# Moving the last 64 rows of a Gram product onto column tiles of TensorE, and its column sums onto four narrower ones

## The chip, the cores and the metric

The kernel runs on one core of a Trainium2 chip. Of its engines, TensorE multiplies matrices and writes the products to a memory called PSUM; VectorE, ScalarE and GpSimd work by element, and VectorE and ScalarE copy results out of PSUM; SyncE's queue issues transfers between memories (DMA). The metric is the device time of one execution in microseconds (us).

## The reference, cut to what matters

```python
B, S, D, H, F = 1, 2048, 576, 32, 4608          # Dh = D // H = 18
xn = layernorm(x)
q, k, v = split(xn @ wqkv)                      # by head
pq, pk = phi(q), phi(k)                         # phi(t) = (t+1 if t > 0 else exp(t)) + 1e-6
kv  = einsum("bhsd,bhse->bhde", pk, v)
z   = einsum("bhsd->bhd", pk)
o   = einsum(pq, kv) / (einsum(pq, z) + 1e-6)
out = x + o @ wo + (gelu(xn @ w_gate) * (xn @ w_up)) @ w_down
```

The kernel does not form v. It uses pk^T v = (pk^T xn) wv. So it accumulates the Gram product G = xn^T pk (576 x 576) over 16 token tiles of 128 tokens, and multiplies by wv later (kv stage). The stretch in which k and pk are computed, one token tile after another, with a part of G accumulated alongside, is called the K stage; a query unit is five matmuls that compute a piece of q. The sum of pk over tokens, z, is one more row of such a product, with a column of ones for xn.

## The kernel before

576 rows are four blocks of 128 and a last block of 64. The column of ones follows the 64, so the last block has 65 weight columns. A matmul takes weights of up to 128 columns (`lhsT`); a block of 65 leaves half the columns of the array empty and takes as long (0.25 us per token tile for 577 columns of pk in three pieces, by the prediction's reading below, where two full pieces with 577 columns take 2 x 0.1235).

```python
G_A = {   # row block: (bank, column, first column of pk, width); runs inside the K stage
    0: [(0, 0, 0, 288), (1, 0, 288, 289)],
    1: [(2, 0, 0, 288), (3, 0, 288, 289)],
    4: [(0, 288, 0, 224), (1, 289, 224, 223), (2, 288, 447, 130)],
}
G_B = {2: [(5, 0, 0, 288), (6, 0, 288, 289)], 3: [(0, 0, 0, 288), (1, 0, 288, 289)]}

def g_accumulate(n, pieces):
    for kt, ps_ in pieces.items():
        j0, m = (kt * P, P) if kt < 4 else (D, HP + 1)
        for b, col, d0, w in ps_:
            nc.tensor.matmul(ps_all[:m, b, col:col + w], lhsT=xn[:, n, j0:j0 + m], rhs=pk[:, n, d0:d0 + w], ...)

# ... after the K stage:
for n in range(NS): g_accumulate(n, {2: G_B[2]})
g_copy(4, ...); g_copy(0, ...); g_copy(1, ...)
# ... the last query steps, q_unit(12)
for n in range(NS): g_accumulate(n, {3: G_B[3]})
g_copy(2, ...); g_copy(3, ...)
q_unit(13)
z_stage(2, 3)       # spreads z over each head's rows, for the denominators
kv_stage(6, 5)      # G times wv
```

Then follow row-tiled pairs (two matmuls over 64 rows of the array side by side): query units, gate and up, and three pairs for the denominators (`den_pair`). A pair swaps its two PSUM banks halfway; an empty instruction on another queue, a "turn", passes the word. For the denominators that queue is SyncE's.

Of the kernel before, what the change touches and what calls it, by code (L numbers as in the profile page):

```python
# [8 lines left out]
ACT = mybir.ActivationFunctionType  # L9
ALU = mybir.AluOpType  # L10
BF16 = mybir.dt.bfloat16
F32 = mybir.dt.float32
# [3 lines left out]
P = 128  # L16
HP = 64
S = 2048
D = 576
# [3 lines left out]
NS = S // P  # L23
# [4 lines left out]
HALF = D // 2  # L28
KT = 5
# [3 lines left out]
CR = 7 * DH  # L33
EPS_LN = 1e-5
EPS_ATT = 1e-6
# [2 lines left out]
WDS = 3  # L38
NWARM = 38
TD = 4  # L40
XW = 642
PKW = 578


class _Ring:
# [11 lines left out]
def kernel(  # L57
# [11 lines left out]
    nc = tc.nc  # L69
# [8 lines left out]
    const = ctx.enter_context(tc.tile_pool(name="const", bufs=1))  # L78
# [6 lines left out]
    ps_all = psum.tile([P, 8, 512], F32, name="ps_all")  # L85
# [10 lines left out]
    apool = attn_cm.__enter__()  # L96
# [5 lines left out]
    wqkv_sb = apool.tile([P, KT, 3 * D], BF16, name="wqkv_sb")  # L102
# [4 lines left out]
    def load_w(which, on=nc.sync):  # L107
        c = slice(which * D, (which + 1) * D)
        on.dma_start(wqkv_sb[:, 0:4, c], A_wqkv[0:512, c].rearrange("(kt p) c -> p kt c", p=P))
        on.dma_start(wqkv_sb[0:HP, 4, c], A_wqkv[512:576, c])  # L110
        if which == 0:
            on.dma_start(wq_lo[HP:P, :], A_wqkv[512:576, c])

    nc.scalar.preload_act_table_set("natural_log_exp_and_others")  # L114
    load_x(0, 1)
# [3 lines left out]
    nc.vector.memset(wqkv_sb[HP:P, 4, :], 0.0)  # L119
    nc.vector.memset(wqkv_sb[0:1, 0, D:D + 2], 0.0)  # L120
    load_w(1, nc.scalar)

    ident = const.tile([P, P], BF16, name="ident")
# [29 lines left out]

    pk = h_store[:, 0:NS * PKW].rearrange("p (n d) -> p n d", n=NS)
    wg_bufs = _Ring([fpool.tile([P, 4, GUB * P], BF16, name=f"wg{i}") for i in range(NWBUF)])
# [5 lines left out]
    def load_gu(i, part):  # L161
# [15 lines left out]


    xn = apool.tile([P, NS, XW], BF16, name="xn")
    nc.gpsimd.memset(xn[:, :, 640:641], 1.0)  # L180
    nc.gpsimd.memset(pk[:, :, D:D + 1], 1.0)

    bmask = const.tile([P, CR], F32, name="bmask")
    bm3 = bmask[:].rearrange("p (h e) -> p h e", e=DH)
# [2 lines left out]
        out=bm3, in_=bm3, compare_op=ALU.is_ge, fill=0.0,  # L187
# [3 lines left out]
        out=bm3, in_=bm3, compare_op=ALU.is_ge, fill=0.0,  # L191
        base=DH - 1, pattern=[[DH, 7], [0, DH]], channel_multiplier=-1,
    )
    g_sb = apool.tile([P, KT, D], BF16, name="g_sb")
    nc.gpsimd.memset(g_sb[HP:P, 4, :], 0.0)

    zsel = const.tile([P, CR], BF16, name="zsel")
    nc.gpsimd.memset(zsel[:], 0.0)
    nc.gpsimd.memset(zsel[HP:HP + 1, :], 1.0)

    mv = persist.tile([P, NS, nc.vector.BN_AGGR_DIM], F32, name="mv")
    rstd = persist.tile([P, NS], F32, name="rstd")
# [36 lines left out]
    def k_bank(n, hf):  # L239

        return hf if n == 1 else 5 + hf
# [9 lines left out]
    def phi_tile():  # L251
        return awork.tile([P, D], F32, name="phi_e", tag="phi_e", bufs=6)


    k_e = {}

    def k_part(n, hf):
        if n not in k_e:
            k_e[n] = phi_tile()
        hs = slice(hf * HALF, (hf + 1) * HALF)  # L260
        return ps_all[:, k_bank(n, hf), :HALF], k_e[n][:, hs], pk[:, n, hs]

    def k_relu(n, hf):
        ps, e, _ = k_part(n, hf)
        nc.scalar.activation(out=e, in_=ps, func=ACT.Relu, scale=-1.0)  # L265

    def k_exp(n, hf):
        _, e, _ = k_part(n, hf)
        nc.scalar.activation(out=e, in_=e, func=ACT.Exp, scale=-1.0)  # L269

    def k_sum(n, hf):
        ps, e, out_ = k_part(n, hf)
        nc.vector.scalar_tensor_tensor(out=out_, in0=ps, scalar=0.0, in1=e, op0=ALU.max, op1=ALU.add)  # L273
# [1 line left out]


    G_A = {
        0: [(0, 0, 0, 288), (1, 0, 288, 289)],
        1: [(2, 0, 0, 288), (3, 0, 288, 289)],
        4: [(0, 288, 0, 224), (1, 289, 224, 223), (2, 288, 447, 130)],  # L280
    }
    G_B = {2: [(5, 0, 0, 288), (6, 0, 288, 289)], 3: [(0, 0, 0, 288), (1, 0, 288, 289)]}
    eps_sum = const.tile([P, KT], F32, name="eps_sum")

    def g_accumulate(n, pieces):
        for kt, ps_ in pieces.items():
            j0, m = (kt * P, P) if kt < 4 else (D, HP + 1)
            for b, col, d0, w in ps_:
                nc.tensor.matmul(  # L289
                    ps_all[:m, b, col:col + w], lhsT=xn[:, n, j0:j0 + m], rhs=pk[:, n, d0:d0 + w],  # L290
                    start=(n == 0 and col == 0), stop=(n == NS - 1), skip_group_check=True,
                )



# [2 lines left out]
    LO, HI = slice(0, HP), slice(HP, P)  # L298
# [37 lines left out]
    def q_unit(i):  # L336
        sc, c = divmod(i, NCH)
        rows = DH * HCH[c]
        q0 = DH * HOFF[c]
        ps = ps_all[:rows, q_banks.next(), :]  # L340
        for kt in range(KT):
            nc.tensor.matmul(  # L342
                ps, lhsT=wqkv_sb[:, kt, q0:q0 + rows], rhs=xnT[:, kt, sc * SC:(sc + 1) * SC],
                start=(kt == 0), stop=(kt == KT - 1),
            )
        q_out[i] = ps
# [57 lines left out]
    def mask_pair(dst, b4, b1):  # L404

        nc.vector.tensor_tensor(
            out=dst[:CR, 0:4, :], in0=ps_all[:CR, b4, 0:4 * CR].rearrange("p (c d) -> p c d", c=4),
            in1=bmask[:CR, :].unsqueeze(1).to_broadcast([CR, 4, CR]), op=ALU.mult,
        )
        r4 = DH * HCH[4]  # L410
        nc.vector.tensor_tensor(
            out=dst[:r4, 4, :r4], in0=ps_all[:r4, b1, 0:r4], in1=bmask[:r4, :r4], op=ALU.mult,
        )

    def chunk_out(c, b4, b1):
        rows = DH * HCH[c]
        return ps_all[:rows, b4, c * CR:c * CR + rows] if c < 4 else ps_all[:rows, b1, 0:rows]

    def z_stage(b4, b1):
        for c in range(NCH):  # L420
            rows = DH * HCH[c]
            nc.tensor.matmul(
                chunk_out(c, b4, b1), lhsT=g_sb[:, 4, c * CR:c * CR + rows], rhs=zsel[:, :rows],
                start=(c in (0, 4)), stop=True, skip_group_check=True,
            )
        mask_pair(zrep, b4, b1)

    def kv_stage(b4, b1):

        for kt in (0, 1, 4, 2, 3):  # L430
            for c in range(NCH):
                rows = DH * HCH[c]
                nc.tensor.matmul(  # L433
                    chunk_out(c, b4, b1), lhsT=wqkv_sb[:, kt, 2 * D + c * CR:2 * D + c * CR + rows],
                    rhs=g_sb[:, kt, c * CR:c * CR + rows],
                    start=(kt == 0 and c in (0, 4)), stop=(kt == 3), skip_group_check=True,
                )
        mask_pair(kvT, b4, b1)

# [29 lines left out]
    def den_norm(sc, c, q, pieces):  # L469
# [30 lines left out]
        (lambda n: k_sum(n, 0), [9.00, 16.55, 13.07, 15.61, 18.43, 21.08, 23.93, 26.99, 30.05]),  # L500
        (lambda n: k_sum(n, 1), [10.83, 11.19, 13.68, 16.19, 18.79, 21.44, 24.29, 27.35, 30.41]),
        (lambda n: g_accumulate(n, G_A), [11.96, 17.36, 18.24, 20.21, 21.09, 23.07, 26.12, 29.18, 32.24]),
    ]

# [27 lines left out]
    todo += [(4.0, lambda n: nc.vector.memset(x_sb[0:1, n, 0:2], 0.0), 4)]  # L532
    todo += [(4.01, lambda n: load_x(n, 4), n) for n in (4,)]
    todo += [(4.02, lambda n: load_w(0), 0)] + [(4.03, lambda n: load_x(n, 4), n) for n in (8, 12)]
    todo.sort(key=lambda x: x[0])

# [2 lines left out]
        step(n)  # L539


    def g_copy(kt, pieces, on):

        m = P if kt < 4 else HP + 1
        eps = eps_sum[:m, kt:kt + 1]
        b, col, _, w = pieces[kt][-1]
        nc.vector.tensor_scalar_mul(out=eps, in0=ps_all[:m, b, col + w - 1:col + w], scalar1=EPS_ATT)
        for (b, col, d0, w), eng in zip(pieces[kt][::-1], on):
            w = min(w, D - d0)
            out_, in_ = g_sb[:m, kt, d0:d0 + w], ps_all[:m, b, col:col + w]  # L550
            if eng is nc.scalar:
                nc.scalar.activation(out=out_, in_=in_, func=ACT.Identity, bias=eps, scale=1.0)
            else:
                nc.vector.tensor_scalar_add(out=out_, in0=in_, scalar1=eps)


    load_w(2)
    for i in range(NWBUF):
        load_gu(i, 0)
        load_gu(i, 1)  # L560
    for n in range(NS):
        g_accumulate(n, {2: G_B[2]})
    g_copy(4, G_A, (nc.vector, nc.scalar, nc.vector))
    g_copy(0, G_A, (nc.scalar, nc.vector))
    g_copy(1, G_A, (nc.scalar, nc.vector))
    for _, step, n in todo[tail:]:
        step(n)
    q_unit(12)
    for step in (q_exp1, q_min, q_max):
        step(12)  # L570
    for n in range(NS):
        g_accumulate(n, {3: G_B[3]})
    g_copy(2, G_B, (nc.scalar, nc.vector))
    g_copy(3, G_B, (nc.scalar, nc.vector))
    q_unit(13)
    z_stage(2, 3)
    kv_stage(6, 5)
    for step in (q_exp1, q_min, q_max):
        step(13)
# [161 lines left out]
```

## Time and profile before

| | kernel before |
|---|---|
| time, median of 3 (range) | 523.57 us (523.47 to 523.83) |
| span of the profiled run | 521.7 us |
| TensorE busy | 99% of the span |
| Gram product after the K stage | two rows of the chain, 4.75 us (with one token tile of the K stage) and 4.00 us |
| first Gram row after the K stage to the row-tiled pairs | 65.78 - 53.20 = 12.58 us |

The view that this document uses most is the chain of work that ended last, in order of time. Each row is a stretch that the next had to wait for: start, length, what, and how many instructions. I call the 12.58 us of the last line the **edited stretch**: all that the change does for TensorE after the K stage lies in it.

### The profile page before, as it was taken

What the parts mean: (1) busy time and instruction counts of PE and PEld (TensorE: products, weight loads), DVE (VectorE), ACT (ScalarE), POOL (GpSimd) and SP (SyncE); (2) the same over time, 40 slices, a digit from 0 to 9 for tenths busy, and PEclk for the clock granted to TensorE, in tenths of its full rate; (3) what the DMA queues carried; (4) which work ended last, traced back from release to release, by engine and by line L of the source; (5) the groups of instructions that cost most, each with busy time, mean ns of one, the idle gap of its engine ahead of it and who ended that gap; (6) DMA issues with size and microseconds to landing.
All of it is one profiled execution on the core that took longest, in us unless ns stands there. A gap on an engine that the chain in (4) does not pass through costs nothing.

```text
span 521.7 us, 10641 instructions
## 1 busy us (share of the span) xinstructions
PE 516.1 (99%) x4498; PEld 313.5 (60%) x4498; DVE 250.9 (48%) x436; ACT 143.1 (27%) x293; POOL 35.2 (7%) x55
## 2 busy tenths in 40 slices
PE   7999999999999999999999999999999999999997
PEld 6777755555587754444577744444777544445775
DVE  7996565876358323433388133333584233433101
ACT  6898442332320013323200032232000123322000
POOL 2021000211001100000012000000011000000000
PEclk9999999999999999999999999999999999999999
DMA  8334609899500045555300155555100355440000
GB/s 279 62 64 118 154 25 264 254 269 266 157 12 13 13 124 155 144 156 160 93 13 13 41 166 145 155 156 155 29 23 13 103 161 158 140 134 2 13 11 24
DMA packets 106282, 57.89 MB, mean 111 GB/s; under 512 B 13370, under 2 KB 105722, under 8 KB 106234
## 3 DMA queue, kind: packets, MB, share of 16 engines
q1 hardware_dynamic: 105626, 56.55, 38.8%
q8 instruction: 35, 0.57, 0.5%
q10 hardware_dynamic: 608, 0.66, 0.4%
q14 instruction: 13, 0.11, 0.1%
HBM read 52.86 MB, written 2.36 MB: 106 GB/s over the span
## 4 chain that ended last, share of the span: by engine, by line
PE 97%; DMA 1%; ACT 1%; DVE 0%; issue 0%
PE ps_all L313 55%; PE ps_all L677 27%; PE ps_all L289 4%; PE ps_all L682 4%; PE ps_all L245 3%; PE ps_all L342 3%; DMA wqkv_sb<-in_A_wqkv_dram 1%; PE ps_all L451 1%; PE ps_all L433 0%; PE ps_all L659 0%; ACT xnT L234 0%; ACT L114 0%; ACT phi_e L265 0%; ACT phi_e L269 0%; DVE hT L273 0%; DVE res L685 0%
## 5 line engine op out<-in xcount | busy, mean ns | idle before, releaser
L313 PE MATMUL ps_all<-xnT,wg 64*128 64x512 bf16 x1152 | 272.6, 376 | 0.0
L313 PE MATMUL ps_all<-xnT,wu 64*128 64x512 bf16 x1152 | 271.8, 376 | 0.0
L648 DVE TENSOR_TENSOR hT<-ps_all,gl 128x512 bf16<-128x512 f32 x144 | 99.5, 691 | 161.9 <-ACT gl L647 161.2
L647 ACT ACTIVATE gl<-ps_all 128x512 f32<-128x512 f32 x144 | 86.1, 598 | 314.3 <-PE ps_all L313 297.4
L313 PEld LDWEIGHTS <-wu 64*128 64x128 bf16 x1152 | 108.3, 94 | 66.3
L313 PEld LDWEIGHTS <-wg 64*128 64x128 bf16 x1152 | 108.3, 94 | 66.1
L677 PE MATMUL ps_all<-wd_sb,hT 128*128 128x288 bf16 x1152 | 147.0, 286 | 0.0
L677 PEld LDWEIGHTS <-hT 128*128 128x128 bf16 x1152 | 112.3, 98 | 30.6 <-issue 1.3
L475 DVE RECIPROCAL den_sb<-den_sb 126x128 f32<-126x128 f32 (+1 forms) x80 | 68.3, 911 | 0.5
L685 DVE TENSOR_TENSOR res<-ps_all,x_sb 128x288 bf16<-128x288 f32 x32 | 14.7, 458 | 88.0 <-PE ps_all L682 88.0
L313 PE MATMUL ps_all<-xnT,wr 64*128 64x512 bf16 x288 | 55.1, 376 | 0.0
L478 POOL TENSOR_TENSOR pqT<-pqT,den_sb 126x512 bf16<-126x512 bf16 (+3 forms) x25 | 24.2, 966 | 317.3 <-DVE den_sb L475 279.4
L682 PE MATMUL ps_all<-m_sb,pqT 126*128 126x288 bf16 (+1 forms) x160 | 24.9, 285 | 0.0
L313 PEld LDWEIGHTS <-wr 64*128 64x128 bf16 x288 | 14.4, 94 | 16.9 <-issue 0.7
L245 PE MATMUL ps_all<-wqkv_sb,xnT 128*128 128x288 bf16 x160 | 22.5, 286 | 0.9 <-DMA wqkv_sb<-in_A_wqkv_dram 0.8
L289 PE MATMUL ps_all<-hT,xn 128*128 128x288 bf16 (+4 forms) x176 | 22.4, 275 | 0.0
L289 PEld LDWEIGHTS <-xn 128*128 128x128 bf16 (+1 forms) x176 | 17.5, 102 | 4.1
L245 PEld LDWEIGHTS <-xnT 128*128 128x128 bf16 x160 | 15.4, 98 | 6.9 <-issue 1.4
L682 PEld LDWEIGHTS <-pqT 126*128 126x128 bf16 (+1 forms) x160 | 15.5, 97 | 4.1
L342 PE MATMUL ps_all<-xnT,wqkv_sb 128*126 128x512 bf16 (+1 forms) x70 | 17.4, 378 | 0.0
L273 DVE SCALAR_TENSOR_TENSOR hT<-ps_all,phi_e 128x288 bf16<-128x288 f32 x32 | 13.2, 450 | 4.6 <-ACT phi_e L269 4.0
L265 ACT ACTIVATE phi_e<-ps_all 128x288 f32<-128x288 f32 x32 | 12.9, 410 | 3.6 <-PE ps_all L245 2.1
(68 smaller groups left out, 173.8 us busy)
## 6 DMA issues: line engine op xcount, KB each, us to landing
wg<-in_B_w_gate_dram SPq DMA_DIRECT2D x72, 256.0 KB, 2.9
wu<-in_B_w_up_dram SPq DMA_DIRECT2D x72, 256.0 KB, 3.5
wd_sb<-in_B_w_down_dram SPq DMA_DIRECT2D x12, 432.0 KB, 4.6
wr<-in_B_w_gate_dram SPq DMA_DIRECT2D x72, 32.0 KB, 2.7
wr<-in_B_w_up_dram SPq DMA_DIRECT2D x72, 32.0 KB, 3.1
out_dram<-res SPq DMA_DIRECT2D x15, 144.0 KB, 1.8
x_sb<-in_A_x_dram SPq DMA_DIRECT2D x3, 576.0 KB, 7.1
wqkv_sb<-in_A_wqkv_dram SPq DMA_DIRECT2D x2, 576.0 KB, 4.7
```

The source lines that it names most:

```text
L245: nc.tensor.matmul(ps_all[:, k_bank(n, hf), :HALF], lhsT=xnT[:, kt, n * P:(n + 1) * P], rhs=wqkv_sb[:, kt, D + hf * HALF:D + (hf + 1) * HALF],
L273: nc.vector.scalar_tensor_tensor(out=out_, in0=ps, scalar=0.0, in1=e, op0=ALU.max, op1=ALU.add)
L289: nc.tensor.matmul(ps_all[:m, b, col:col + w], lhsT=xn[:, n, j0:j0 + m], rhs=pk[:, n, d0:d0 + w], start=(n == 0 and col == 0), stop=(n == ...
L313: return nc.tensor.matmul(self.outs[i], lhsT=self.lhs(i, rows, kt), rhs=self.rhs(i, rows, kt), start=start, stop=stop, skip_group_check=True,)
L342: nc.tensor.matmul(ps, lhsT=wqkv_sb[:, kt, q0:q0 + rows], rhs=xnT[:, kt, sc * SC:(sc + 1) * SC], start=(kt == 0), stop=(kt == KT - 1),)
L475: nc.vector.reciprocal(out=d[:, h:h + P], in_=d[:, h:h + P])
L478: nc.gpsimd.tensor_tensor(out=pqT[:rows, c, cols], in0=pqT[:rows, c, cols], in1=d, op=ALU.mult)
L647: nc.scalar.activation(out=gl[:], in_=ps_all[:, b[0], :], func=ACT.Gelu_apprx_tanh)
L648: nc.vector.tensor_tensor(out=hT[:, GUB * k + i, :], in0=ps_all[:, b[1], :], in1=gl[:], op=ALU.mult)
L677: nc.tensor.matmul(acc, lhsT=hT[:, f, j * P:(j + 1) * P], rhs=wd_sb[:, f, hs], start=(f == 0), stop=False,)
L682: nc.tensor.matmul(acc, lhsT=pqT[:rows, c, ts_], rhs=m_sb[:rows, c, hs], start=False, stop=(c == NCH - 1),)
L685: nc.vector.tensor_tensor(out=res[:, hs], in0=acc, in1=x_sb[:, n, hs], op=ALU.add)
```

## The change

The intent: the array time that 65 of 128 columns left unused. The third row block takes the place of the last one inside the K stage. The last 64 rows come after the K stage, on two column tiles of 64: one takes the first 288 columns of pk, the other the second 288, at the same time. z can't ride along as a 65th column, so it gets matmuls of its own, with ones as weights, on four column tiles of 32: tile g takes token tiles g, g+4, and so on. The four partial sums are added in the z stage, by four rows of ones in place of one.

```diff
-    4: [(0, 288, 0, 224), (1, 289, 224, 223), (2, 288, 447, 130)],
+    2: [(0, 288, 0, 224), (1, 289, 224, 223), (2, 288, 447, 132)],
     }
-G_B = {2: [...], 3: [...]}
+G_B = {3: [(5, 0, 0, 288), (6, 0, 290, 289)]}
+def g_last(bank):
+    for n in range(NS):
+        for hf in range(2):
+            nc.tensor.matmul(
+                ps_all[hf * HP:(hf + 1) * HP, bank, 0:HALF + 1], lhsT=xn[:, n, 4 * P:4 * P + HP],
+                rhs=pk[:, n, PK0[hf]:PK0[hf] + HALF + 1],
+                start=(n == 0), stop=(n == NS - 1), skip_group_check=True,
+            )
+def z_sums(b0):
+    for n in range(NS):
+        g = n % 4
+        for hf in range(2):
+            nc.tensor.matmul(
+                ps_all[g * ZQ:(g + 1) * ZQ, b0 + hf, 0:HALF], lhsT=z_ones[:], rhs=pk[:, n, PK0[hf]:PK0[hf] + HALF],
+                start=(n < 4), stop=(n >= NS - 4), skip_group_check=True,
+            )
...
-    for n in range(NS):
-        g_accumulate(n, {3: G_B[3]})
-    g_copy(2, G_B, (nc.scalar, nc.vector))
-    g_copy(3, G_B, (nc.scalar, nc.vector))
+    g_last(0)
+    z_sums(1)
+    g_copy(3, ...)
+    g_copy(4, ...)
+    z_copies(1)          # one half on ScalarE, one on VectorE
     q_unit(13)
     z_stage(2, 3)
```

Cut here: layout of pk with a column of ones behind each half, a second copy of 64 rows of wv (one transfer more on SyncE's queue), the memsets, the kv stage's order.

## The prediction

> **What bounds the kernel now.** I read first the busy shares on the page of the kernel before, then its chain of work that ended last, then the same chain in order of time around the place that the change edits.
>
> ```profile
> PE 516.1 (99%) x4498; PEld 313.5 (60%) x4498; DVE 250.9 (48%) x436; ACT 143.1 (27%) x293; POOL 35.2 (7%) x55
> ...
> PE 97%; DMA 1%; ACT 1%; DVE 0%; issue 0%
> ```
>
> TensorE is busy in 99% of the span and makes up 97% of the chain. The chain in order of time, from the end of the K stage (each row: start, length, what):
>
> ```profile
> 52.12 1.08 PE ps_all L342 x5
> 53.20 4.75 PE ps_all L289 x39
> 57.95 1.08 PE ps_all L342 x5
> 59.02 4.00 PE ps_all L289 x32
> 63.02 1.08 PE ps_all L342 x5
> 64.10 0.26 PE ps_all L422 x5
> 64.36 1.43 PE ps_all L433 x25
> 65.78 24.31 PE ps_all L313 x223
> ```
>
> L289 is the Gram product, L342 a query unit, L422 the z stage, L433 the kv stage, L313 the row-tiled pairs. Each row starts where the last one ends: no other engine and no DMA has a link here, and from 12.04 us on every link of the K stage is TensorE too (rows of L245, L289 x7 and L342 only). So the time answers to TensorE's own issue time, nanosecond for nanosecond, unless the change puts a wait on that chain.
>
> From the rows I take slot lengths, which are what counts (a matmul's own duration, 286 ns, overlaps its neighbours). Ten 288-column matmuls of L245 take 1.23 us: 0.1225 us each. The 32 of the row at 59.02 (16 of 288 and 16 of 289 columns) take 4.00: 0.125 each. Five of 512 columns take 1.08: 0.215 each. The row-tiled pairs take 24.31 / 223 = 0.109 each, half of a 512-column slot, so two row tiles really run side by side.
>
> The groups of L289 by shape show what the last 64 rows of the Gram matrix cost: three matmuls per token tile with 65 weight columns.
>
> ```profile
> L289 PE MATMUL ps_all<-hT,xn 128*128 128x289 bf16 x64 | 16.6, 287 | 0.0
> L289 PE MATMUL ps_all<-hT,xn 128*128 128x288 bf16 x64 | 16.6, 286 | 0.0
> ...
> L289 PE MATMUL ps_all<-hT,xn 128*65 128x223 bf16 x16 | 4.2, 259 | 0.0
> L289 PE MATMUL ps_all<-hT,xn 128*65 128x224 bf16 x16 | 4.1, 258 | 0.0
> L289 PE MATMUL ps_all<-hT,xn 128*65 128x130 bf16 x16 | 3.5, 222 | 0.0
> ```
>
> The chain gives seven L289 matmuls per token tile 0.745 us. Four of them are full pieces at about 0.1235; the other three are left with 0.745 - 0.494 = 0.25 us per token tile, 4.0 us in all. That half-empty array time is what the change is after.
>
> **What the Trainium skill says.** (1) "TensorEngine Tiling (Array Packing)", Tiling Modes, Key Properties: tiles run loads and matmuls in parallel, but changing the tiling mode drains TensorE. The trace agrees for row tiles: in the timeline of TensorE at the end of the first gate/up stage the last pair starts at 255.14, and the first full-array matmul only at 255.45, 0.31 us later instead of one slot of 0.213, so about 0.10 us goes to the switch, and the next slot is 10 ns long as well.
>
> ```profile
> 255.14 0.38 PE L313 MATMUL ps_all<-xnT,wg 64*128 64x512 bf16 x1
> 255.45 0.66 PE L677 MATMUL ps_all<-wd_sb,hT 128*128 128x288 bf16 x4
> ```
>
> (2) Same page, Restrictions: column tiling goes without fast weight load. The trace of before has no column tile; its 126-column loads show 135 ns against 98 for 128 columns, and at the switch at 65.7 us, with 126-column weights, the second pair came 0.26 us after the first instead of 0.213. (3) "TensorE: Matmul & The Clock Gate", Part 3, The mechanism: matmuls start and end in program order, "strict FIFO, no reordering". Before can't show that, since its row tiles always alternate. (4) Same page, Part 3, Measured speedup vs the span model: three 32-column tiles gave 2.38x, so column tiles do overlap. Nothing in this trace tests it.
>
> **The change part by part.**
>
> K stage. The three 65-column matmuls per token tile (577 columns together) leave, and the third row block takes their place in three pieces of 224, 223 and 132 columns: 579 columns at 128 weight columns. Two columns more at 0.1225/288 us is under 1 ns per token tile, 0.01 us in all. Weight loads stay hidden, as those of L245 are. Change: about 0.
>
> After the K stage. Before: two blocks of 32 full matmuls, 4.00 + 4.00 us. After: one block of 32 (the fourth row block, 4.00 us) and in place of the other:
> - the last 64 rows, 32 matmuls of 289 columns on two 64-column tiles that alternate strictly: 16 pair slots of 0.126 = 2.0 us.
> - z, 32 matmuls of 288 columns on 32-column tiles. The order is token tile outside, half inside, so each tile gets two matmuls in a row: tile 0, 0, 1, 1, 2, 2, 3, 3. If starts keep program order, the second matmul of a tile has to wait for the first, and only the next tile's first can join it. That makes pairs, not fours: 17 slots of 0.1225 = 2.1 us. Were the four tiles truly filled, it would be 8 slots and a little, 1.0 to 1.1 us.
> - three more changes of mode: full array to 64 columns, to 32, and back to full with 126-column weights. The trace's price is 0.10 to 0.14 each; I take 0.39 in all.
>
> Sum with pairs in z: 2.0 + 2.1 + 0.39 = 4.5 us in place of 4.0, so 0.5 us longer. Sum with four z tiles at once: 2.0 + 1.05 + 0.39 = 3.45, so 0.55 us shorter.
>
> The tail. The z stage now needs z copied out of PSUM, which starts only when the z sums end. The query unit of 1.08 us lies between. Call T the end of the last z slot. The last matmul's own end is some 0.17 later (286 minus a slot). The copies then take one length of 288 columns from PSUM on each engine: 0.50 on ScalarE and 0.52 on VectorE, as in the timeline of VectorE before:
>
> ```profile
> 63.06 0.16 DVE L547 TENSOR_SCALAR eps_sum<-ps_all 128x1 f32<-128x1 f32 x1 [1.53 <-PE ps_all L289]
> 63.25 0.52 DVE L554 TENSOR_SCALAR g_sb<-ps_all,eps_sum 128x288 bf16<-128x288 f32 x1
> 64.36 0.68 DVE L406 TENSOR_TENSOR zrep<-ps_all,bmask 126x504 bf16<-126x504 f32 x1 [0.59 <-PE ps_all L422]
> ```
>
> That puts z at T + 0.75 with a handover; the z stage is due at T + 0.14 + 1.08 = T + 1.22. Nearly 0.5 us to spare, and the copies of row blocks three and four lie before, under the z sums. VectorE waited 1.53 us there before, so there is room. I expect no wait of TensorE.
>
> The start. GpSimd gets some small memsets more and one less (by the instruction order: four one-row writes of 0.20 us where there was one, a column of ones, a 128x32 block). Before, it was done with them at 3.6 us and then idle until its first copy at 5.8, so some 0.8 us more is hidden. One more weight transfer of 64 rows joins a queue whose data is needed after 60 us. The copies out of PSUM of the third row block become four, about 0.35 us more on ScalarE, which stands idle 2.1 us soon after. All cost nothing.
>
> **Rivals.** *A: z runs on four tiles at once*, because each tile takes its second matmul into a queue of its own and the next tile's matmul passes. For it: the change is written as four tiles, evidently with this in mind, and full-array matmuls are already handed over back to back. Against: the skill's in-order statement. 523.0 us. *B: column tiles don't overlap here*, as both streams read all 128 partitions where row tiles read halves, or the slower weight loads show. Without any overlap 32 x 0.1255 + 32 x 0.1225 + 0.39 - 4.0 = 4.3 us longer, 527.9; against it, the skill's 2.38x, and the weight loads take a few tens of ns of a slot that has 122. Partly so (a slot of 0.15 for 0.125) would add about 0.8 us: 524.8. *C: a wait ahead of the z stage* takes back what the array saves: 0.5 us of slack speaks against; a late ScalarE would cost perhaps 0.3. *D: the K stage changes speed*, since 128 weight columns get the fast load that 65 didn't: the 130-column piece has a slot of about 60 ns; at most 3 ns per token tile, 0.05 us.
>
> **Range and chances.** I give pairs in z 0.6 (524.05), A 0.27 (523.0), and B wholly or in part 0.13. Between the two likely cases, nearer the first: **523.9 us**. The range 522.8 to 524.7 holds both, with the 0.2 us by which runs differ. Even full B is under 1% slower, so within 2% is all but certain: 0.98, and 0.01 on either side.
>
> **What would show it.** In the changed trace, the 64-column matmuls should fill about 2.0 us, starting in pairs; the z matmuls about 2.1 us, in pairs one slot apart (in fours and 1.05 us if A holds; singly if B). Their neighbours should show three gaps of about 0.1 us. The z stage should start with no idle of TensorE, the copies of z ending about 0.5 us ahead of it. The K stage should keep its 3.06 us per token tile, and everything from the row-tiled pairs to the end should only be shifted. I am wrong if the shift comes from elsewhere (first weights, the K stage, a wait at the z stage), or if column tiles don't pair.

## The result, and the profile after

| | before | after |
|---|---|---|
| median of 4 runs (range) | 523.52 us (523.07 to 523.83) | 523.19 us (522.86 to 525.08) |
| ratio | | 1.0002 (0.9977 to 1.0027) |
| again, five rounds: median | 523.67 us | 523.15 us (522.65 to 523.32) |
| ratio | | 0.9990 (0.9977 to 1.0002) |

(In the set of five rounds, the kernel before ran nine times.) A ratio is the mean time of one kernel's fast runs over that of the other's of the same rounds, so it is not quite the ratio of the medians. The first is above 1 although the median fell: one run of four took 525.08 us. That run happens to be the profiled one. Both intervals hold 1, so by time alone no difference is proved; the traces tell more.

The page of the kernel after, busy shares and the chain by engine:

```profile
PE 516.0 (99%) x4530; PEld 309.3 (59%) x4530; DVE 251.0 (48%) x437; ACT 143.6 (27%) x295; POOL 35.9 (7%) x61
...
PE 94%; DMA 3%; ACT 1%; SPq 1%; issue 0%; DVE 0%
```

SPq (SyncE's queue) is new on the chain, and DMA has 3% in place of 1%. The chain in order of time, over the edited stretch (L302 Gram, L311 the last 64 rows, L322 z, L380 query unit, L460 z stage, L470 kv stage, L351 row-tiled pairs):

```profile
54.22 4.72 PE ps_all L302 x39
58.94 1.08 PE ps_all L380 x5
60.02 2.10 PE ps_all L311 x32
62.12 1.11 PE ps_all L322 x30
63.23 1.22 PE ps_all L380 x5
64.45 0.26 PE ps_all L460 x5
64.71 1.43 PE ps_all L470 x25
66.14 9.87 PE ps_all L351 x90
```

The stretch is 66.14 - 54.22 = 11.92 us, **0.66 us shorter**. 2.10 + 1.11 stand where 4.00 stood, and the query unit behind them has 0.14 more for the last change of mode. No other engine is on the chain inside it. (z is 32 matmuls; two have no place in the merged row.)

So this trace should have been shorter by 0.66 us and was longer by 1.6 (spans before rounding). What TensorE waited for, in this trace (total, times, longest):

```profile
PE ps_all L258 <- DMA wqkv_sb<-in_A_wqkv_dram: 1.2, 1, 1.2
PE ps_all L351 <- SPq L360: 0.9, 1, 0.9
PE ps_all L258 <- DMA xnT<-xn: 0.5, 1, 0.5
```

The kernel before, in its first trace, has of these only the first, and 0.8 in place of 1.2; in its second trace (run null) that wait is 1.3, so it is not the change's. The second is the turn of the first denominator pair, which SyncE sent late at 89.1 us; the third is a DMA transpose in the K stage, at 48 us. Both lie outside the edited lines. By the start times of the matmuls, the 1.6 adds up: the first weights come 0.32 us later, the transpose costs 0.70 and the turn 1.08, the stretch saves 0.66, and the end, of which more below, costs 0.19. The first two questions for experiments are therefore: how do 32 z matmuls fit in 1.11 us, when I had expected 2.1? And do these pauses belong to the change?

The copies of z, from the timeline of ScalarE and of VectorE in the kernel after:

```profile
63.28 0.50 ACT L329 ACTIVATE z_sb<-ps_all,eps_z 128x288 bf16<-128x288 f32 x1 [0.17 <-PE ps_all L322]
```

```profile
63.14 0.51 DVE L590 TENSOR_SCALAR g_sb<-ps_all,eps_sum 64x288 bf16<-64x288 f32 x1 [0.56 <-ACT g_sb L588]
63.57 0.44 DVE L330 TENSOR_SCALAR z_sb<-ps_all 128x288 bf16<-128x288 f32 x1
```

z is ready at 63.57 + 0.44 = 64.01 us, ahead of the z stage's row at 64.45. The spare time is a little less than predicted, because VectorE's copy of the last 64 rows waited 0.56 us for ScalarE, which was reading the other half of the same PSUM bank. That the shared bank is why the program has this wait is likely, but not tested.

### The profile page after: what moved, and what is told of

Read it like the earlier page. It is cut to its first block, busy times and chain, and to the rows that moved or that the text cites. A ratio compares the mean times of both kernels' runs of the same rounds, so it can differ in the third digit from the quotient of the medians.

```text
span 523.4 us, 10713 instructions
## 1 busy us (share of the span) xinstructions
PE 516.0 (99%) x4530; PEld 309.3 (59%) x4530; DVE 251.0 (48%) x437; ACT 143.6 (27%) x295; POOL 35.9 (7%) x61
## 4 chain that ended last, share of the span: by engine, by line
PE 94%; DMA 3%; ACT 1%; SPq 1%; issue 0%; DVE 0%
PE ps_all L351 53%; PE ps_all L717 27%; PE ps_all L722 4%; PE ps_all L258 3%; PE ps_all L302 3%; PE ps_all L380 3%; DMA wo<-in_A_wo_dram 1%; DMA wqkv_sb<-in_A_wqkv_dram 1%; DMA xnT<-xn 1%; PE ps_all L488 1%; PE ps_all L311 0%; SPq L177 0%; ACT phi_e L278 0%; PE ps_all L470 0%; PE ps_all L699 0%; SPq L176 0%
## 5 line engine op out<-in xcount | busy, mean ns | idle before, releaser
L351 PE MATMUL ps_all<-xnT,wg 64*128 64x512 bf16 x1152 | 272.5, 376 | 0.0
L351 PE MATMUL ps_all<-xnT,wu 64*128 64x512 bf16 x1152 | 271.9, 376 | 0.0
L351 PEld LDWEIGHTS <-wu 64*128 64x128 bf16 x1152 | 108.3, 94 | 67.9
L351 PEld LDWEIGHTS <-wg 64*128 64x128 bf16 x1152 | 108.3, 94 | 67.7
L351 PE MATMUL ps_all<-xnT,wr 64*128 64x512 bf16 x288 | 54.7, 376 | 0.0
L351 PEld LDWEIGHTS <-wr 64*128 64x128 bf16 x288 | 14.1, 94 | 17.2 <-issue 0.7
L302 PE MATMUL ps_all<-hT,xn 128*128 128x288 bf16 (+4 forms) x144 | 18.2, 273 | 0.0
L380 PE MATMUL ps_all<-xnT,wqkv_sb 128*126 128x512 bf16 (+1 forms) x70 | 17.4, 379 | 0.0
L302 PEld LDWEIGHTS <-xn 128*128 128x128 bf16 x144 | 13.9, 97 | 3.3
```

What stands on the lines that cost most here:

```text
L302: nc.tensor.matmul(ps_all[:, b, col:col + w], lhsT=xn[:, n, kt * P:(kt + 1) * P], rhs=pk[:, n, p0:p0 + w], start=(n == 0 and col == 0), st ...
L351: return nc.tensor.matmul(self.outs[i], lhsT=self.lhs(i, rows, kt), rhs=self.rhs(i, rows, kt), start=start, stop=stop, skip_group_check=True,)
L380: nc.tensor.matmul(ps, lhsT=wqkv_sb[:, kt, q0:q0 + rows], rhs=xnT[:, kt, sc * SC:(sc + 1) * SC], start=(kt == 0), stop=(kt == KT - 1),)
```

## The experiments

Twelve kernels ran. All gave correct results, and all ratios are against the kernel before in the same rounds. Where an expectation says "stretch" with 12.7, 12.0 or 11.0 us, it means the edited stretch counted from the first matmul's start to the first pair's start, which is 0.1 more than between the rows of the chain.

### The changed kernel again, and the kernel before against itself

No edit.

> The changed kernel once more, unaltered, for the spread of its times and a second trace. The first trace holds three pauses of TensorE that have nothing to do with the edited lines: first weights 0.32 us later, 0.70 us at 47 us for a DMA transpose, 1.03 us at 88 us for a turn signal on the SyncE queue. Theory 1 (chance: the DMA was slow in that one run): the pauses are mostly gone, the time is 523.0, ratio to the kernel before 0.9985 to 0.9995, and the stretch from the third Gram block to the row-tiled pairs is 0.65 us shorter again. Theory 2 (the change causes them, by its one added weight transfer or by later starts): the pauses come back at the same places and the mean of the times is at or above 523.6.

> The kernel before against itself, in the same five rounds: the noise. Theory 1 expects a ratio of 1.000 with an interval of about plus or minus 0.0007, and that a run with a pause for DMA (over 524.5) can turn up here too. Theory 2 expects no such run here.

Measured: the changed kernel 523.15 us, ratio 0.9990 (0.9977 to 1.0002). The kernel before against itself 523.90, ratio 1.0010 (0.9997 to 1.0023), with one run of 525.29. So two programs that are the same can differ by 0.1% in the mean, and the gain asked for is 0.13%. In the trace of the changed kernel the edited stretch is again 11.92 us (52.87 to 64.79); in that of the kernel before 12.59 (53.67 to 66.26). The gain in the stretch is a property of the change: it came again as 0.67 us. The transpose pause did not come back. The turn came late again, with SyncE waiting first (its own waits, in the changed kernel's second trace):

```profile
SPq L174 <- DMA wo<-in_A_wo_dram: 0.9, 1, 0.9
```

By the waits in the program, SyncE issues a new transfer only when the one eight places before it has landed; here that was the attention output weights, `wo`. TensorE's pause at the pair was 0.4 us by the waits, and the pair finished 0.66 us late by the matmuls' start times. Theory 1 is half right: the other pauses went, this one stayed.

### z in the order of the four tiles

```diff
-        for n in range(NS):
-            g = n % 4
-            for hf in range(2):
+        for n0 in range(0, NS, 4):
+            for hf in range(2):
+                for n in range(n0, n0 + 4):
+                    g = n % 4
```

> The z sums in the order tile 0, 1, 2, 3 for one half, then 0, 1, 2, 3 for the other, so that program order itself fills the four column tiles. If matmuls of a free tile pass those that wait for a busy one (theory 1), the z sums already ran in fours and stay at 1.0 to 1.1 us on the chain. If the trace's fours come from something else in the order, for instance that two matmuls in a row on one tile run at once because they go to two banks (theory 2), this order changes them: the slot of four should then hold 8 matmuls or fewer than 4, and the z sums take other than 1.0 us.

Measured: 523.32 us, ratio 0.9993 (0.9979 to 1.0006). The z row of the chain, L323 in this kernel, is 1.10 us against 1.11, the stretch 11.91 (53.35 to 65.26):

```profile
61.25 1.10 PE ps_all L323 x30
```

Order made no difference here. So in the kernel after, where each tile gets two matmuls in a row, the tiles were as full as when the order itself fills them.

### z in blocks of eight on one tile

```diff
-            g = n % 4
+            g = n // 4
-                    start=(n < 4), stop=(n >= NS - 4), skip_group_check=True,
+                    start=(n % 4 == 0), stop=(n % 4 == 3), skip_group_check=True,
```

> Each 32-column tile gets four token tiles in a row, so eight matmuls one after the other on the same tile. Theory 1a (passing with a deep window of 30 or so matmuls): z sums stay at 1.0 to 1.1 us. Theory 1b (passing with a short window of a few matmuls): between 2 and 3.8 us, tiles overlapping only near the change of tile. Theory 2 (strict program order): 29 slots of 0.1225, 3.55 us. A wait for the copies of z then follows only as in the kernel after, so the time moves by the same amount: 523.0, 524 to 525.7, or 525.5.

Measured: 525.02 us, ratio 1.0024 (1.0009 to 1.0039). The chain:

```profile
59.78 2.10 PE ps_all L311 x32
61.88 2.63 PE ps_all L322 x32
```

2.63 us, and the stretch is 13.44. This is the short window of theory 1b. The size can be worked out: without the change of mode, about 0.13, 2.5 us are 20 slots of 0.1225 (20 x 0.1225 = 2.45). Twenty slots come out if matmuls are handed over in program order, but each tile can hold four, one running and three waiting. Tile 0 works alone for four slots; then its last four are all inside, and tile 1's first can pass to its own tile. So each of the three further tiles adds four slots: 8 + 3 x 4 = 20. The start times of the single matmuls in the trace agree: four alone, then pairs 5 to 19 ns apart, then four alone at the end.

A rival fits as well: one window of four waiting matmuls for all tiles together, from which any may start whose tile is free, and which refills as they leave. Counted by slots, it too gives 20 here, 8 for the original order and for the run before, and 28 for the next run. What the runs show is that a few matmuls can wait while others pass; whether each tile holds its own (three besides the one running) or all tiles share four places stays open. Four in a row on each tile would tell: by the same counting, two rounds of that (32 matmuls) take 8 slots with places for each tile and 11 with the shared window. It was not run.

### The last 64 rows with 16 in a row on one tile

```diff
-        for n in range(NS):
-            for hf in range(2):
+        for hf in range(2):
+            for n in range(NS):
```

> The last 64 rows with the half outside and the token tile inside: 16 matmuls in a row on the first 64-column tile, then 16 on the second. The run with z in blocks of eight took 4 slots of one, 16 of two overlapping: as if program order held, but each tile kept up to 4 matmuls (one running, three waiting), so that the next tile can start when the one before has 4 left. That theory expects 16 + 16 - 4 = 28 slots of 0.1235 = 3.46 us in place of 2.0, so 1.45 us longer, 524.5. A window that counts all matmuls, of 8 x 3 or more, would give 2.0; strict program order 31 slots, 3.8 us.

Measured: 525.02 us, ratio 1.0025 (1.0011 to 1.0039). The chain:

```profile
59.00 3.61 PE ps_all L311 x32
62.60 1.11 PE ps_all L322 x31
```

28 slots of 0.1235 are 3.46 and the change of mode about 0.12, so 3.58 was to be expected by the theory of four places, and 3.61 came. Strict order (31 slots) would have given 3.95 by the same sum, a deep window 2.10. The theory was made from one run and held in another of other tile width and run length. (The shared window gives 28 slots too.)

### All of z on one tile

```diff
-            g = n % 4
+            g = 0
-    for g in range(P // ZQ):
-        nc.gpsimd.memset(zsel[g * ZQ:g * ZQ + 1, :], 1.0)
+    nc.gpsimd.memset(zsel[0:1, :], 1.0)
+    nc.gpsimd.memset(z_sb[:], 0.0)
```

(and start/stop flags, eps and copies to match)

> All z sums on one 32-column tile, so 32 matmuls one after the other. Any theory: 32 slots of 0.1225 = 3.92 us in place of 1.02, 2.9 us longer on the chain; 526.0. What it tells is what column tiles are worth, and whether anything hides it.

Measured: 526.08 us, ratio 1.0044 (1.0031 to 1.0057); as expected.

```profile
61.05 4.06 PE ps_all L322 x32
```

Two matmuls of one tile do take turns, a slot each. Together with the 1.11 us above this shows that four tiles really ran side by side in the changed kernel, so that the first matmul of tile 1 started ahead of the second of tile 0, out of program order. It also shows that this stretch goes into the time in full: 2.95 us more on the chain, 2.9 more in the median (526.08 - 523.15; by the two ratios, 1.0044 and 0.9990, 2.8).

### The 64 rows on 32-column tiles too

```diff
             for hf in range(2):
-                nc.tensor.matmul(
-                    ps_all[hf * HP:(hf + 1) * HP, bank, 0:HALF + 1], lhsT=xn[:, n, 4 * P:4 * P + HP],
+                for q in range(2):
+                    r0 = hf * HP + q * ZQ
+                    nc.tensor.matmul(
+                        ps_all[r0:r0 + ZQ, bank, 0:HALF + 1], lhsT=xn[:, n, 4 * P + q * ZQ:4 * P + (q + 1) * ZQ],
```

> The last 64 rows on 32-column tiles too, two for each half (64 matmuls in place of 32), so that z follows with no change of mode between. If four tiles run side by side as in z, the slots are the same 16 of 0.1235 and one switch of 0.09 to 0.11 us is gone: the stretch takes 11.9 us against 12.0. If weight loads (four of 32 columns for each slot) begin to show, it is longer, up to 12.5. The time can't tell so little; the trace does. The program is 128 rows longer than before, so where SyncE waits may shift again.

Measured: 523.14 us against 523.94, ratio 0.9986 (0.9973 to 1.0000), the lowest ratio of all. The chain (L313 the 64 rows, L324 z):

```profile
59.05 2.09 PE ps_all L313 x63
61.14 0.99 PE ps_all L324 x30
```

The stretch is 11.79 us (53.25 to 65.04): 0.13 less than in the kernel after. That is the price of one change of mode, a little above the 0.09 to 0.11 expected. Four weight loads in each slot cost nothing: this row is 2.09 us against 2.10. It beats both kernels in the trace's stretch; in time it can't be told from the kernel after.

### The turn of the denominator pairs on GpSimd's queue

```diff
-            nc.sync, first=(0,), then=(0,),
+            nc.gpsimd, first=(0,), then=(0,),
```

> The changed kernel, with the turn signal of the three denominator pairs sent by GpSimd's queue in place of SyncE's, nothing else. All three traces of the changed order show TensorE pausing 0.4 to 1.0 us at the first denominator pair, some 21.9 us after the first row-tiled pair, for a turn on the SyncE queue, which is held up in issuing weight transfers; the two traces of the kernel before show none. Theory 1 (the pause is a real part of the changed kernel's time and comes from SyncE being late): no pause there, time 522.4 to 522.8, ratio 0.9975 to 0.9985. Theory 2 (the weights themselves are late, and the turn only shows it first): the pause comes back some microseconds later as a wait for weights, and the time stays at 523.1.

Measured: 523.47 us, ratio 0.9997 (0.9985 to 1.0010). In the trace the pause at the pair is gone, although SyncE waited 0.6 us for `wo` there, and no wait for weights takes its place. So the pause comes from SyncE's late turn, as theory 1 has it, as far as one trace can show. The time expected from it did not come: this trace has a transpose pause of 0.3 us by the waits, and one of five runs took 525.20. A missed expectation: the pause comes in some runs only, and next to the others it is too small to be seen in the times.

### Does the length of the instruction stream do it?

The kernel before with 32 more matmuls in the warm-up, and the kernel after with 32 fewer:

```diff
-    spin(NWARM)                 # the kernel before, 128 columns each
+    spin(NWARM + 32)            # 64 columns each
```

```diff
-    spin(NWARM)                 # the kernel after
+    spin_wide(9)                # 512 columns each
-    todo += [(t, spin, count) for t, count in [(5.80, 3), (6.20, 5), (8.50, 2)]]
+    todo += [(5.80, spin_wide, 1), (6.20, spin, 4), (8.50, spin, 2)]
```

> The kernel before with 32 more warm-up matmuls at the start, all of them 64 columns wide in place of 128, so that the TensorE program is as long (64 rows more) as the changed kernel's when the row-tiled pairs begin; the Gram product is untouched. In the traces the instruction transfers of 16 KB fall at 9.4 us after the first row-tiled pair in the kernel before, and at 5.6 and 20.6 us in the changed one. Theory 1a (the place of the instruction transfers, moved by the number of instructions, is what makes SyncE late): the pause of 0.4 to 1.0 us at the denominator pair appears here too, and the time is 523.9 to 524.6, if the start itself isn't moved by more than 0.1. Theory 1b (the change makes it late in another way, such as the added weight transfer, or chance): no pause, 523.5 to 523.8.

> The changed kernel with its warm-up made of 512-column matmuls, so many fewer that the TensorE program is exactly as long (8998 rows) as that of the kernel before; it is the converse of the padded kernel. So far all eight traces of programs 64 rows longer show SyncE waiting 0.4 to 1.0 us for the attention output weights at its third weight block, four of them a pause of 0.4 to 0.7 us for a DMA transpose in the K stage, and three a pause at the first denominator pair; the two traces of the kernel before show none of it. Theory 1 (the length of the instruction stream sets it): no such wait, no such pauses, the edited stretch 0.67 us shorter, time 522.7 to 523.0, no run above 524. Theory 2 (it belongs to the added weight transfer and to chance): the wait of SyncE is there as before, time 523.1, now and then 525.

Measured: the kernel before, padded, 524.63 us, ratio 1.0028 (1.0008 to 1.0048), with two runs of 526.8. The interval lies above 1, so the padded kernel is slower; the profiled run took 524.40, and no trace shows what made the two long ones long. The time is at the edge of what theory 1a expected, the pauses are theory 1b's: a transpose pause, none at the pair, and a SyncE wait for `wo`:

```profile
SPq L172 <- DMA wo<-in_A_wo_dram: 0.4, 1, 0.4
```

The kernel after, trimmed to the length of the kernel before, 523.34, ratio 0.9991 (0.9978 to 1.0005), stretch 11.92. Its SyncE wait:

```profile
SPq L181 <- DMA wo<-in_A_wo_dram: 1.0, 1, 1.0
```

The theory of the length falls: at the old length the wait is as long as ever. The added transfer of the change is not needed either, since the padded kernel before hasn't got it and waits as well. All twelve traces other than the two of the kernel before have this wait (0.2 to 1.0 us). But it does not always stop TensorE. By the matmuls' start times, the first denominator pair is held up by 1.08 us in the first trace of the changed kernel, 0.66 in its second, 0.45 with z in the order of the tiles, and 0.15, 0.15 and 0.09 with z on one tile, in the trimmed kernel and with the 64 rows on 32-column tiles; in the other traces by nothing. (The waits given above are shorter, since each counts from the modelled end of the matmul before.) Whether two traces without it are chance, I can't say.

### z summed on GpSimd

```diff
+    def z_add(n):               # z_acc (f32) += pk[n]; the last one writes bf16
+        nc.gpsimd.tensor_tensor(
+            out=(z_acc16 if n == NS - 1 else z_acc)[:, 0:w], in0=pk[:, 0, 0:w] if n == 1 else z_acc[:, 0:w],
+            in1=pk[:, n, 0:w], op=ALU.add,
+        )
-        for n in range(NS): ...  # 32 matmuls
+        for hf in range(2):      # 2 matmuls on two 64-column tiles, rhs=z_acc16
+        (z_add, [x_, 17.0, 18.0, 19.2, 20.4, 21.90, 24.76, 27.82, 30.88]),
```

> The token tiles of phi(k) are summed on GpSimd, which is idle in nine tenths of the K stage, in 15 additions of 128 x 578; TensorE sums the one remaining tile over the partitions with two 64-column matmuls side by side. That leaves out 30 matmuls of z and one change of mode: 1.02 + 0.09 - 0.13 = about 1.0 us less on the chain than in the kernel after, and the program is 4 rows longer than before. If GpSimd is in time and does not hold up VectorE: the stretch from the third block to the row-tiled pairs takes 11.0 us (12.7 before, 12.0 after), and 521.8 to 522.2. Rival: VectorE, busy in 84% of the K stage, slows by sharing with GpSimd, and the K stage grows by 0.5 us or more: 522.5 to 524.

Measured: 529.08 us, ratio 1.0099 (1.0085 to 1.0113). The stretch is 10.93 us between the rows of the chain, one microsecond less, as hoped. But the K stage grew by some 7 us; TensorE's longest wait there:

```profile
PE ps_all L389 <- DVE pqT L435: 4.9, 6, 0.9
```

TensorE waited for the query sum on VectorE, that for GpSimd's eps addition, and that stood behind a sum which waited for VectorE. The second try puts each sum one token tile later:

```diff
-        (z_add, [x_, 17.0, 18.0, 19.2, 20.4, 21.90, 24.76, 27.82, 30.88]),
+        (z_add, [x_, 17.5, 19.5, 20.6, 21.90, 24.76, 27.82, 30.88, 33.93]),
```

> The GpSimd sums again, each addition put one token tile later in GpSimd's order, so that it waits for nothing and the eps addition of the query unit doesn't stand behind it. In the run before, the K stage grew by 7.1 us, TensorE waiting six times for the query sum of VectorE, which waited for GpSimd's eps addition, which stood behind a sum of 1.28 us that itself waited for VectorE; the edited stretch was 11.02 us as hoped. Theory 1 (only that ring of waits made it slow): K stage back at 40.4 us, stretch 11.0, time 522.0 to 522.4. Theory 2 (VectorE itself: its copies of 128 x 64 took 344 ns in place of 181 and its normalisation 488 in place of 419 while GpSimd added): VectorE, already busy 34 of 41 us, gets 0.25 us a token tile more, so the K stage grows by 0.5 to 3 us: 522.7 to 525.

Measured: 523.88 us, ratio 1.0002 (0.9988 to 1.0015). The ring is gone and the stretch is 10.93 us (54.84 to 65.77), but theory 2 holds. The normalisation on VectorE, in the K stage, in the kernel after and in this one (last figures: busy us, mean ns):

```profile
L229 DVE TENSOR_SCALAR xn<-x_sb,mv,rstd 128x576 bf16<-128x576 bf16 x12 | 5.0, 419 | 0.0
```

```profile
L233 DVE TENSOR_SCALAR xn<-x_sb,mv,rstd 128x576 bf16<-128x576 bf16 x11 | 6.7, 610 | 0.0
```

It took 610 ns in place of 419. From the first Gram matmul to the first Gram block behind the K stage, this trace needs 1.4 us more than those without a pause (41.8 against 40.4 us by the start times), and VectorE now makes up most of the chain from 17.6 us on. Waits of TensorE for VectorE and for a transpose (0.8 and 0.3 us) are part of it; the rest is not split further. What the array saved, the K stage took back.

## Why the prediction was right or wrong

**The time.** 523.9 was predicted, with a range of 522.8 to 524.7; 523.19 came, and 523.15 in the second set. The range held, and "within 2%" was never in doubt; but the range was made to hold both likely cases, so that it held says nothing for the mechanism. The sign was wrong where it can be told: the edited stretch became 0.66 us shorter, where 0.5 longer was given as likelier. In the time no change is proved; the medians fell.

**What bounds the kernel: right.** TensorE's own issue time sets the end. With all of z on one tile, 2.95 us on the chain became 2.9 us of time.

**The step that failed** is "If starts keep program order, the second matmul of a tile has to wait for the first, and only the next tile's first can join it. That makes pairs, not fours: 17 slots of 0.1225 = 2.1 us." The runs showed four at a time, 1.11 us with its change of mode: rival A, which had 0.27. A busy tile does not stop the others at once: a few matmuls can wait, and others pass them. The counts of slots in two runs fit four places for each tile, and as well four waiting places shared by all; which of the two it is stays open. I had named this very possibility ("each tile takes its second matmul into a queue of its own") and put it below the page's sentence on order, of which the prediction itself says that the kernel before can't show it.

**The other terms were well sized.** The 64 rows: 2.0 us plus a share of the switches, 2.10 measured. Three changes of mode: 0.39 expected; left over in the three rows are 2.10 - 16 x 0.1235 = 0.12, 1.11 - 8 x 0.1225 = 0.13 and 1.22 - 1.08 = 0.14, together 0.39. The case with four z tiles was put at 0.55 us less (its three terms give 3.44, written as 3.45), and 0.66 was measured. Of the difference, 0.03 is in the Gram row (4.72 in place of 4.75) and the rest in slots slightly shorter than taken.

**The K stage: right.** Where no DMA pause falls into it, the way from the first Gram matmul to the block behind the K stage is 40.4 us in the traces of both kernels.

**The tail: right in what counts.** No wait at the z stage. The spare time was sized at nearly 0.5 us; by the rows it is 64.45 - 64.01 = 0.44, less by about 0.15 when counted to the first z matmul's start. The lost part comes from VectorE's wait of 0.56 us for ScalarE's copy.

**"Everything from the row-tiled pairs to the end should only be shifted": up to the last matmul in five of eleven traces, to the end in none.** From the first pair's start to the last matmul's, 452.76 us pass in all three traces with the old order and in five of the eleven with the new one. In the other six only the first denominator pair is late, by the 0.09 to 1.08 us given above; that part of the gain is given back in such runs. What makes SyncE late more in the later traces than in the two of the kernel before is open: length of the program and the added transfer were tried, and neither explains it.

**One cost was missed: the added transfer is not free at the end.** The prediction listed it among what costs nothing. From the last matmul's start to the end of the span, the three traces with the old order take 3.26 or 3.27 us, all eleven with the new one 3.45 to 3.47. The program ends with SyncE checking, in a fixed order, the eight semaphores by which its transfers report. They are used in turn, so 343 transfers in place of 342 put the last store on another one: checked in the second of six instructions, not in the sixth. Its landing is awaited there, until 2.42 us after the last matmul's start in the changed kernel's second trace (2.46 in the first of the kernel before), and four more checks of some 0.06 us each follow. So 0.19 of the 0.66 us is given back in every run that was traced, and some 0.47 is left; between the medians 0.33 and 0.52 came in the two sets. The traces show where the time goes; no run takes the transfer away alone.

## What to carry to other kernels

Fill column tiles with no more than a few consecutive matmuls for each tile: two in a row ran as well as perfect alternation, eight in a row cost 1.5 us of stretch here, three to seven were not run, and the count of slots for orders like these can be worked out beforehand with four places (for others, such as four in a row, the two open theories differ). Put matmuls of equal tile size side by side, since each change of mode costs 0.12 to 0.14 us. When a gain is 0.1% of the time, read it from the stretch in the trace, which repeats to 0.01 us, because runs of one and the same kernel differ by more; then follow the gain to the end of the span, where a part of it can be lost again. And before giving work to an idle engine, see which engine it shares its way to memory with.

## What the Trainium skill lacked or had wrong

- "TensorE: Matmul & The Clock Gate", Part 3, The mechanism, has matmuls in strict program order with no reordering. Here, matmuls for another column tile passed waiting ones: 32 with two in a row on each of four tiles took 1.11 us, against 4.06 on one tile. The passing is limited: eight in a row gave 2.63 us (20 slots), sixteen in a row 3.61 us (28 slots), which fits four places for each tile, and as well four waiting places shared by all. No page gives such a number for matmuls.
- "TensorEngine Tiling (Array Packing)", Key Properties, says that a change of mode drains TensorE but gives no price: 0.12 to 0.14 us each on the chain, and leaving one out saved 0.13.
- The same page, Restrictions, says that column tiling goes without fast weight load. No cost of it showed: with four 32-column loads in each slot the row took 2.09 us, with two 64-column loads 2.10.
- "SBUF — State Buffer", Who interferes with whom, says that GpSimd and some VectorE instructions, tensor_scalar among them, can lock each other out of a shared port pair. The trace agrees in kind: 419 ns became 610 for the normalisation while GpSimd added. The two slowdowns that the page quotes are not given for this mix.
- No page among those used here tells of SyncE's queue being late as a reason for TensorE to wait; an empty turn behind weight transfers cost 1.08, 0.66 and 0.45 us by start times in three traces. Nor does one tell that the number of transfers decides how many checks follow the last store: 0.19 us here.
